# Dealing out the next group's x operands singly, loading two weight sets before the fixed tail, and loading the first group's weights a step sooner

## The chip, the cores and the metric

The kernel runs on one core of a Trainium2 chip. The metric is the device time of one execution, in microseconds (us). In this text TensorE is PE, VectorE is DVE, ScalarE is ACT, GpSimd is POOL, and SP is the engine that issues the DMA transfers. Each engine has a queue of its own and works through it in its program's order; an instruction that waits for a semaphore holds all that stands behind it on that engine.

## The reference

```python
# q, k, v: (8, 12, 448, 64) f32;  w_in: (768, 2048);  w_out: (2048, 768)
scores = (q @ k.T) / sqrt(64) - log(448)
attn = sigmoid(scores) @ v
x = attn.transpose(0, 2, 1, 3).reshape(8 * 448, 12 * 64)   # 3584 tokens x 768
h = x @ w_in
r = maximum(h, 0)
out = (r * r) @ w_out
```

## The kernel before

The attention comes first (until about 249.7 us) and leaves x in DRAM (`xd`), transposed. Then comes the MLP over four groups of tokens, `GROUPS`: three of 2 x 512 tokens and a last one of 2 x 256, here called groups 0 to 3. Each group has two matrix products, `gemm1` (x by w_in, L566) and `gemm2` (relu squared, by w_out, L678). Both are done by a 2 x 2 block scheme with seven products in the place of eight, numbered 1 to 7, whose operands are sums and differences of blocks.

Every f32 operand is split into a rounded high half and a low rest: `split_to` (L344) casts on ACT (the row `L345 ACT CAST`) and subtracts on DVE (`L347 DVE TENSOR_TENSOR`). A product of two split operands takes three matmuls (`product`, L558): high by high, high weights by low x, low weights by high x. So a weight set or an x operand can be used only when its DMA has landed, its cast is done on ACT and, for the second or third matmul, its subtraction is done on DVE.

**gemm1** runs 56 steps, each of one product n and one chunk i of eight, written (n, i), of 9 matmuls. `STEPS` gives their order. Weights come in kinds: A for products 1 and 2, B for 6 and 7, C for 3 and 5, D for 4. `w1C_1_6` is kind C, group 1, chunk 6; the trace drops the numbers and calls it `w1C`. Its PE rows write `ha`, `hb` and `hc`. The last ten steps, the tail, are (1,7), (5,6), (2,7), (6,7), (3,6), (7,7), (5,7), (4,6), (3,7), (4,7). In groups 1 to 3 they stand in a fixed order written out by hand, with a list `work` of loads (`load`), splits of weights (`halve`) and splits of operands (`operand`) for the first product of `gemm2`, each behind a numbered tail step (L661 to L674). A loop ahead of it (L658) loads and halves A, B and C of chunk 7 and D of chunk 6. C of chunk 6, which (5,6) needs as the tail's second step, is loaded and halved in line, just ahead of that step.

**gemm2** runs its products in the order 1, 2, 6, 7, 5, 4, 3, each of 72 matmuls. Its PE rows write `oa`, `ob` and `oc`. While a product runs, the operands and weights of the next are made: `operand(n, j)` (L687) for j = 0 to 3. The operands of product 3 are called `o3_0` to `o3_3` here; the trace writes the halves of any product's j-th operand as `o_0h`, `o_0l` and so on, and the blocks that they are split from as `g`.

**The next group's x** is loaded and combined by `x_operands` (L356). It makes loads of four blocks, 11, 12, 22 and 21 (each an `x` tile of two thirds and a `y` tile of one third), and a dictionary of eleven pieces: 1, 2, t1, t2, 6, t3, 7, 5, 3, t4, 4. The numbers are splits of that product's operand, the t's are differences on DVE. Some of them overwrite a loaded block, so their order matters. `ahead` (L764) issues the loads and all eleven pieces at the start of product 4's part of the program, ahead of `operand(3, 0)`.

What sets the order: the attention and all of `gemm1` of group 0 are written in a fixed order. There, `between` gives the work behind each step: loads of weights (`load_first`) six steps ahead of their use, halves three steps ahead, and three deferred conversions of w_out chunks (`deferred`, L184), each with four loads, ACT and DVE work, and seven stores to DRAM (`store`, L210) at its end. `gemm2` and the first 46 steps of `gemm1` in groups 1 to 3 are ordered by a scheduler that goes by the order in which the program issues work, so what is issued first has the better place on ACT, DVE and SP.

The tiles come from pools with fixed numbers of buffers: 35 of two columns (`op2`: x tiles, operands, g blocks), 12 of one column (`op1`: y tiles, snaps, outputs) and 7 wide ones for weights (`wide`). A load waits until its buffer is free, so a weight load goes out when PE is done with the set that is seven loads back.

Of the kernel before, what the change touches and what calls it, by code (L numbers as in the profile page):

```python
# [64 lines left out]
PIECES = {7: (1,), 14: (3,), 21: (2,), 22: (6,)}  # L65
T_PIECES = {22: ("t1", "t2"), 23: ("t3",)}
FIRST_W1 = 20
PUTS_FIRST = (9, 17)


@with_exitstack
def sigmoid_attention_relu2_mlp(
# [111 lines left out]
    def deferred(i, at):  # L184


        f, a, s = {}, {}, {}

        def load(n, u, k):
            t = op2(f"fd{n}_{i}").rearrange("p a s -> p (a s)")[:, : 2 * HALF]  # L190
            nc.sync.dma_start(out=t.bitcast(I32), in_=w_out[u][:, k * HALF : (k + 1) * HALF].bitcast(I32))
            f[n] = t.rearrange("p (n w) -> p n w", w=2)

        def block(n):
            return op1(f"b{n}_{i}")[:, :HALF]

        def words(n):
            a[n] = block(n)
            convert_upper(f[n], a[n])
            convert_lower(f[n], a[n])  # L200

        def add_up():
            for n in (5, 6, 7, 3):
                s[n] = block(n)
            nc.vector.tensor_add(out=s[5], in0=a[0], in1=a[4])
            nc.vector.tensor_sub(out=s[6], in0=s[5], in1=a[1])
            nc.vector.tensor_sub(out=s[7], in0=a[1], in1=a[0])
            nc.vector.tensor_sub(out=s[3], in0=a[2], in1=s[6])

        def store():  # L210
            for n, t in (a | s).items():
                if n:
                    nc.sync.dma_start(out=w2[i][:, PLACE[1][n]], in_=t)

        out = []
        for b, (n, u, k) in enumerate(((1, i, 0), (0, i, 1), (4, i + NI, 0), (2, i + NI, 1))):
            out.append((at + 3 * b - 5, lambda n=n, u=u, k=k: load(n, u, k)))
            out.append((at + 3 * b, lambda n=n: words(n)))
            out.append((at + 3 * b + 1, lambda n=n: convert_join(f[n], a[n])))
        out.append((at + 12, add_up))  # L220
        out.append((at + 13, store))
        return out

    def load_weights(src, name):
# [309 lines left out]
    def load_first(i, kind):  # L534
        first[i, kind] = load_w1(0, i, kind)
# [30 lines left out]
    def gemm1(g, ops, weights, between):  # L566

        T = GROUPS[g][1]
        blocks, operands, second = {}, {}, {}
        banks, snaps = {}, {}

        def tile_of(n, i):
            if (n, i // 2) not in blocks:
                blocks[n, i // 2] = op2(f"g{n}_{g}_{i // 2}", n=T)
            return blocks[n, i // 2][:, i % 2]

        def squares(n, i, scalar=False):  # L580
            if i % 2 == 0:
                return
            t = blocks[n, i // 2]
            if scalar:
                if n != "12":
                    nc.scalar.activation(t, t, AF.Relu)
                nc.scalar.activation(t, t, AF.Square)
            else:
                nc.vector.scalar_tensor_tensor(out=t, in0=t, scalar=0.0, in1=t, op0=ALU.max, op1=ALU.mult)

        pending = []

        def squares_later(n, i):

            if g == 0:
                pending.append(lambda: squares(n, i, scalar=True))
            else:
                squares(n, i)

        def flush(count):  # L600
            for _ in range(count):
                pending.pop(0)()

        def snap(k, i):
            s = snaps[k, i] = op1(f"s{k}_{g}_{i}", n=T)
            nc.scalar.copy(out=s, in_=banks["a", i])  # L606

        def run(n, i):
            count = len(pending)
            kind, at = SPOT[n]  # L610
            if (i, kind) not in weights:
                weights[i, kind] = halve_weights(load_w1(g, i, kind))
            k = {1: "a", 6: "a", 5: "a", 3: "a", 7: "b", 4: "b", 2: "c"}[n]
            if n in (1, 7, 2):
                banks[k, i] = bank(f"h{k}_{g}_{i}")[:, :T]
            out = banks[k, i]
            hi, lo = weights[i, kind]
            w = tuple(t[:, at].rearrange("p (c m) -> p c m", m=P) for t in (hi, lo))
            for c in range(NE):
                product(out, w, c, ops[n][c], n in (1, 7, 2) and c == 0, c == NE - 1)  # L620
            if n == 1:
                snap(1, i)
            elif n == 2:
                nc.vector.tensor_add(out=tile_of("11", i), in0=out, in1=snaps[1, i])
                squares("11", i)
            elif n == 6:
                snap(2, i)
            elif n == 5:
                snap(4, i)
                nc.vector.tensor_add(out=tile_of("22", i), in0=banks["b", i], in1=snaps[4, i])  # L630
                squares_later("22", i)
            elif n == 3:
                nc.scalar.activation(tile_of("12", i), out, AF.Relu)
                squares("12", i, scalar=True)
                if i % 2:
                    t, o = blocks["12", i // 2], blocks["11", i // 2]
                    nc.vector.tensor_sub(out=t, in0=t, in1=o)
            elif n == 4:
                nc.vector.tensor_add(out=tile_of("21", i), in0=out, in1=snaps[2, i])
                squares_later("21", i)  # L640
            flush(count)

        def operand(j):
            operands[j] = split(blocks["11", j], f"o1_{g}_{j}", lambda *name: op2(*name, T))

        def load(j):
            second[j] = load_w2(g, 1, j)

        def halve(j):
            halve_weights(second[j])  # L650

        head, tail = STEPS[g > 0][:-TAIL], STEPS[g > 0][-TAIL:]
        for at, (n, i) in enumerate(head):
            run(n, i)
            for work in between.get(at, ()):
                work()
        if g > 0:
            for i, kind in ((NI - 1, "A"), (NI - 1, "B"), (NI - 1, "C"), (NI - 2, "D")):  # L658
                if (i, kind) not in weights:
                    weights[i, kind] = halve_weights(load_w1(g, i, kind))  # L660
        work = [(1, load, 0), (3, load, 1), (4, halve, 0), (5, operand, 0), (6, operand, 1), (7, halve, 1)]  # L661
        if g > 0:
            work.append((0, lambda kind: weights.update({(NI - 1, kind): load_w1(g, NI - 1, kind)}), "D"))
            work.append((4, lambda kind: halve_weights(weights[NI - 1, kind]), "D"))
        with ExitStack() as fixed:
            if g > 0:
                fixed.enter_context(tc.manual_schedule())
            for at, (n, i) in enumerate(tail):
                run(n, i)
                for piece in between.get(len(head) + at, ()):  # L670
                    piece()
                for behind, piece, arg in work:
                    if behind == at:
                        piece(arg)  # L674
        flush(len(pending))
        return blocks, operands, second

    def gemm2(g, blocks, operands1, weights1, ahead):  # L678
# [51 lines left out]
        for j in range(NI // 2):  # L730
            operand(1, j)
        for at, n in enumerate(order):
            if n == 4:
                ahead()
            k = {1: "a", 6: "a", 5: "a", 3: "a", 7: "b", 4: "b", 2: "c"}[n]
            if n in (1, 7, 2):
                for e in range(NE):
# [1 line left out]
            for j in range(NI // 2):  # L739
                if at + 1 < len(order):  # L740
                    operand(order[at + 1], j)
                for e in range(NE):
                    for i in (2 * j, 2 * j + 1):
                        w = tuple(t[:, i % 2].rearrange("p (c m) -> p c m", m=P) for t in weights[n][j])
                        x = tuple(t[:, i % 2] for t in ops[n][j])
                        product(banks[k, e], w, e, x, n in (1, 7, 2) and i == 0, i == NI - 1)
# [14 lines left out]
                    put("21", e, 0, 6)  # L761

    def ahead_of(g):
        def ahead():  # L764
            if g < NG:
                ops[g], pieces = x_operands(g)
                for piece in pieces.values():
                    piece()

        return ahead  # L770

    with tc.manual_schedule():
# [45 lines left out]
            uses.setdefault((i, SPOT[product_][0]), n)  # L818
        for (i, kind), n in uses.items():
            if n >= 10 and (i, kind) not in first:  # L820
                work.append((n - 6, lambda i=i, kind=kind: load_first(i, kind)))
                work.append((n - 3, lambda i=i, kind=kind: halve_weights(first[i, kind])))
        for n, i in enumerate(DEFERRED):
            work += deferred(i, 6 + 11 * n)
        between = {}
# [2 lines left out]
        made = gemm1(0, ops[0], first, between)  # L828
    gemm2(0, *made, ahead_of(1))
    for g in range(1, NG):  # L830
        gemm2(g, *gemm1(g, ops[g], {}, {}), ahead_of(g + 1))


# [35 lines left out]
```

## Time and profile before

| | us |
|---|---|
| median of 3 runs | 1093.89 (1093.74 to 1094.51) |
| profiled execution | 1095.63 |
| its span, first to last instruction | 1093.9 |
| PE busy in it | 1065.7 (97%) |
| DVE busy | 799.9 (73%) |
| ACT busy | 652.9 (60%) |
| POOL busy | 72.9 (7%) |
| mean granted TensorE clock | 0.991 |

The span is what the trace covers; the profiled execution's time has 1.7 us more around it. Matmul ends are modelled, so a PE row's start is what to go by: back to back matmuls start at an even distance, and a larger one is lost time. The granted clock is a share of 2.4 GHz; the other level is 1.2 GHz, which reads 0.5. An idle time with `<-` names what the waiting instruction waited for last.

### The profile page before, as it was taken

What the parts mean: (1) busy time and instruction counts of PE and PEld (TensorE: products, weight loads), DVE (VectorE), ACT (ScalarE), POOL (GpSimd) and SP (SyncE); (2) the same over time, 40 slices, a digit from 0 to 9 for tenths busy, and PEclk for the clock granted to TensorE, in tenths of its full rate; (3) what the DMA queues carried; (4) which work ended last, traced back from release to release, by engine and by line L of the source; (5) the groups of instructions that cost most, each with busy time, mean ns of one, the idle gap of its engine ahead of it and who ended that gap; (6) DMA issues with size and microseconds to landing.
All of it is one profiled execution on the core that took longest, in us unless ns stands there. A gap on an engine that the chain in (4) does not pass through costs nothing.

```text
span 1093.9 us, 16699 instructions
## 1 busy us (share of the span) xinstructions
PE 1065.7 (97%) x6433; PEld 829.9 (76%) x6433; DVE 799.9 (73%) x1009; ACT 652.9 (60%) x910; POOL 72.9 (7%) x42
## 2 busy tenths in 40 slices
PE   9999999999999999979999999899999999999998
PEld 4555555557778888868887888778887888799898
DVE  5999989986776897574554996764555994747696
ACT  7899898885665865443443654533434663545664
POOL 1322322200120000000000000000000000000000
PEclk9999999999999999989999999999999999999999
DMA  9989999964464445533332445543333344556564
GB/s 356 380 298 332 351 391 346 329 218 142 143 233 139 124 121 178 168 96 107 102 101 72 116 129 166 167 123 87 89 100 95 106 124 148 154 165 184 169 194 128
DMA packets 90832, 196.13 MB, mean 179 GB/s; under 512 B 8320, under 2 KB 51712, under 8 KB 90752
## 3 DMA queue, kind: packets, MB, share of 16 engines
q1 hardware_dynamic: 90608, 195.00, 54.8%
q8 instruction: 50, 0.82, 0.3%
q14 instruction: 30, 0.25, 0.1%
q10 hardware_dynamic: 144, 0.07, 0.0%
HBM read 154.14 MB, written 40.89 MB: 178 GB/s over the span
## 4 chain that ended last, share of the span: by engine, by line
PE 62%; DVE 4%; DMA 3%; ACT 1%; issue 1%; SPq 0%; ACTq 0%; DVEq 0%
PE oa L562 20%; PE ha L562 17%; PE hb L562 9%; PE ob L562 6%; PE oc L562 5%; PE hc L562 4%; DMA w<-w 1%; DMA y<-xd 1%; DVE xlt L347 1%; DMA w1C<-w 1%; DVE x L375 1%; DVE yt L347 0%; DVE xl L347 0%; DVE y L347 0%; DVE y L375 0%
## 5 line engine op out<-in xcount | busy, mean ns | idle before, releaser
L347 DVE TENSOR_TENSOR w<-w 128x768 fp32r<-128x768 f32 x112 | 106.5, 953 | 60.3 <-ACT w L345 59.9
L345 ACT CAST w<-w 128x768 fp32r<-128x768 f32 x112 | 93.1, 835 | 92.1 <-DMA w<-w 85.7
L266 ACT ACTIVATE at<-sc 128x896 f32<-128x896 f32 x144 | 119.5, 941 | 6.7 <-PE sc L278 6.7
L606 ACT COPY s<-ha 128x512 f32<-128x512 f32 (+1 forms) x96 | 51.0, 533 | 114.0 <-PE ha L562 111.1
L309 PE MATMUL pav<-at,v 64*64 64x448 f32 x1152 | 118.1, 540 | 0.0
L309 PEld LDWEIGHTS pav<-at,v 64*64 64x64 f32 x1152 | 41.6, 133 | 60.8 <-issue 54.2
L516 DVE TENSOR_TENSOR ql<-x,qh 128x896 fp32r<-128x896 f32 x47 | 72.4, 1580 | 0.0
L562 PE MATMUL oa<-o_0h,w 128*128 128x512 f32 (+1 forms) x192 | 58.5, 379 | 11.6 <-ACT o_0h L345 11.6
L162 POOL TENSOR_TENSOR a<-a,f 128x768 int32<-128x768 int32 x26 | 58.1, 2235 | 163.8 <-DVE a L159 75.2
L347 DVE TENSOR_TENSOR w1A<-w1A 128x768 fp32r<-128x768 f32 x31 | 29.6, 955 | 39.3 <-ACT w1A L345 39.0
L278 PE MATMUL sc<-qh 64*128 64x448 f32 x282 | 54.2, 381 | 2.3 <-DVE xo L341 2.3
L562 PE MATMUL oa<-o_3h,w 128*128 128x512 f32 (+1 forms) x192 | 55.6, 363 | 0.0
L562 PE MATMUL oa<-o_1h,w 128*128 128x512 f32 (+1 forms) x192 | 55.6, 362 | 0.0
L562 PE MATMUL oa<-o_2h,w 128*128 128x512 f32 (+1 forms) x192 | 55.6, 362 | 0.0
L347 DVE TENSOR_TENSOR w1B<-w1B 128x768 fp32r<-128x768 f32 x31 | 30.1, 972 | 33.1 <-ACT w1B L345 33.1
L278 PE MATMUL sc<-qh,ql 64*128 64x448 f32 x282 | 51.5, 362 | 0.4 <-DVE ql L516 0.4
L278 PE MATMUL sc<-ql,qh 64*128 64x448 f32 x282 | 51.4, 361 | 0.0
L562 PEld LDWEIGHTS oa<-o_0h,w 128*128 128x128 f32 x192 | 36.4, 198 | 18.3 <-ACT o_0h L345 12.5
L347 DVE TENSOR_TENSOR w1C<-w1C 128x768 fp32r<-128x768 f32 x32 | 32.3, 1008 | 24.4 <-ACT w1C L345 24.4
L345 ACT CAST w1A<-w1A 128x768 fp32r<-128x768 f32 x32 | 26.7, 834 | 38.2 <-DMA w1A<-w 38.0
L562 PE MATMUL ha<-xht,w1C 128*128 128x512 f32 (+1 forms) x128 | 42.0, 374 | 7.3 <-ACT w1C L345 4.9
L345 ACT CAST w1C<-w1C 128x768 fp32r<-128x768 f32 x32 | 26.7, 835 | 37.0 <-DMA w1C<-w 37.0
(189 smaller groups left out, 2821.6 us busy)
## 6 DMA issues: line engine op xcount, KB each, us to landing
w<-w SPq DMA_DIRECT2D x112, 384.0 KB, 3.4
x<-qk SPq DMA_DIRECT2D x47, 448.0 KB, 6.5
f<-w_in SPq DMA_DIRECT2D x16, 768.0 KB, 9.0
w1A<-w SPq DMA_DIRECT2D x32, 384.0 KB, 3.2
w1B<-w SPq DMA_DIRECT2D x32, 384.0 KB, 3.2
w1C<-w SPq DMA_DIRECT2D x32, 384.0 KB, 3.5
v<-v SPq DMA_DIRECT2D x24, 448.0 KB, 7.0
w<-s SPq DMA_DIRECT2D x26, 384.0 KB, 8.5
```

The lines of the kernel that those rows point to most:

```text
L162: nc.gpsimd.tensor_tensor(out=wb, in0=wb, in1=t.bitcast(I32)[:, :, 0], op=ALU.add)
L266: nc.scalar.activation(at, sc, AF.Sigmoid, bias=NEG_LOG_S, scale=SCALE)
L278: nc.tensor.matmul(sc[:, j], x[kp][rows, 1, ks], x[qp][rows, 0], start=(n == 0), stop=(n == len(passes) - 1),)
L309: nc.tensor.matmul(sums[columns, h], vt[rows, n % 2 * NT + t, columns], at[t][rows, j], start=(t == 0 and (n % 2, h) != (1, 1)), stop=(t = ...
L345: nc.scalar.copy(out=hi, in_=raw)
L347: nc.vector.tensor_sub(out=lo, in0=raw, in1=hi.bitcast(F32))
L375: nc.vector.tensor_sub(out=o, in0=x, in1=y)
L516: nc.vector.tensor_sub(out=xs[n][1], in0=x[n], in1=xs[n][0].bitcast(F32))
L562: nc.tensor.matmul(out, a[:, c], b, start=first and n == 0, stop=last and n == 2, skip_group_check=True)
L606: nc.scalar.copy(out=s, in_=banks["a", i])
```

## The change

Three things are altered.

1. The next group's x. The loads of the four blocks are issued one product sooner, at the start of product 5's part. The eleven pieces no longer come at once. `AHEAD` deals out 1, 2, t1, t2 with 6, t3 and 7, each behind one `operand(3, j)` of product 4's part or one j of product 3's part; `BEHIND` puts 5, 3, t4 and 4 behind steps 0, 2, 4 and 5 of the next `gemm1`.
2. The tail of `gemm1` in groups 1 to 3. The loop ahead of the tail now takes A of chunk 7, C of chunk 6, B of chunk 7 and D of chunk 6. C of chunk 7 is loaded behind tail step 0 and halved behind 3; D of chunk 7 is loaded behind 3 (was 0) and halved behind 6 (was 4). The loads of product 1's first two weight sets of `gemm2` move from behind 1 and 3 to behind 2 and 5, their halves from 4 and 7 to 5 and 8, the two operand splits from 5 and 6 to 6 and 7. These latter moves hold for group 0's tail too.
3. Group 0's weights. Loads go seven steps ahead of their use (was six), halves four (was three), and the deferred conversions' stores go out four steps later.

```diff
--- before.py
+++ after.py
@@ -65,6 +65,10 @@
 PIECES = {7: (1,), 14: (3,), 21: (2,), 22: (6,)}
 T_PIECES = {22: ("t1", "t2"), 23: ("t3",)}
 FIRST_W1 = 20
+
+
+AHEAD = {2: (1,), 3: (2,), 4: ("t1",), 5: ("t2", 6), 6: ("t3",), 7: (7,)}
+BEHIND = {0: (5,), 2: (3,), 4: ("t4",), 5: (4,)}
 PUTS_FIRST = (9, 17)
 
 
@@ -218,7 +222,7 @@
             out.append((at + 3 * b, lambda n=n: words(n)))
             out.append((at + 3 * b + 1, lambda n=n: convert_join(f[n], a[n])))
         out.append((at + 12, add_up))
-        out.append((at + 13, store))
+        out.append((at + 17, store))
         return out
 
     def load_weights(src, name):
@@ -655,13 +659,18 @@
             for work in between.get(at, ()):
                 work()
         if g > 0:
-            for i, kind in ((NI - 1, "A"), (NI - 1, "B"), (NI - 1, "C"), (NI - 2, "D")):
+            for i, kind in ((NI - 1, "A"), (NI - 2, "C"), (NI - 1, "B"), (NI - 2, "D")):
                 if (i, kind) not in weights:
                     weights[i, kind] = halve_weights(load_w1(g, i, kind))
-        work = [(1, load, 0), (3, load, 1), (4, halve, 0), (5, operand, 0), (6, operand, 1), (7, halve, 1)]
+        def load_last(kind):
+            weights[NI - 1, kind] = load_w1(g, NI - 1, kind)
+
+        def halve_last(kind):
+            halve_weights(weights[NI - 1, kind])
+
+        work = [(2, load, 0), (5, load, 1), (5, halve, 0), (6, operand, 0), (7, operand, 1), (8, halve, 1)]
         if g > 0:
-            work.append((0, lambda kind: weights.update({(NI - 1, kind): load_w1(g, NI - 1, kind)}), "D"))
-            work.append((4, lambda kind: halve_weights(weights[NI - 1, kind]), "D"))
+            work = [(0, load_last, "C"), (3, halve_last, "C"), (3, load_last, "D"), *work, (6, halve_last, "D")]
         with ExitStack() as fixed:
             if g > 0:
                 fixed.enter_context(tc.manual_schedule())
@@ -730,8 +739,8 @@
         for j in range(NI // 2):
             operand(1, j)
         for at, n in enumerate(order):
-            if n == 4:
-                ahead()
+            if n == 5:
+                ahead(None)
             k = {1: "a", 6: "a", 5: "a", 3: "a", 7: "b", 4: "b", 2: "c"}[n]
             if n in (1, 7, 2):
                 for e in range(NE):
@@ -739,6 +748,8 @@
             for j in range(NI // 2):
                 if at + 1 < len(order):
                     operand(order[at + 1], j)
+                if n in (4, 3):
+                    ahead((n == 3) * NI // 2 + j)
                 for e in range(NE):
                     for i in (2 * j, 2 * j + 1):
                         w = tuple(t[:, i % 2].rearrange("p (c m) -> p c m", m=P) for t in weights[n][j])
@@ -761,11 +772,14 @@
                     put("21", e, 0, 6)
 
     def ahead_of(g):
-        def ahead():
+        def ahead(at):
             if g < NG:
-                ops[g], pieces = x_operands(g)
-                for piece in pieces.values():
-                    piece()
+                if at is None:
+                    ops[g], made = x_operands(g)
+                    pieces.clear()
+                    pieces.update(made)
+                else:
+                    pieces_of(*AHEAD.get(at, ()))
 
         return ahead
 
@@ -818,8 +832,8 @@
             uses.setdefault((i, SPOT[product_][0]), n)
         for (i, kind), n in uses.items():
             if n >= 10 and (i, kind) not in first:
-                work.append((n - 6, lambda i=i, kind=kind: load_first(i, kind)))
-                work.append((n - 3, lambda i=i, kind=kind: halve_weights(first[i, kind])))
+                work.append((n - 7, lambda i=i, kind=kind: load_first(i, kind)))
+                work.append((n - 4, lambda i=i, kind=kind: halve_weights(first[i, kind])))
         for n, i in enumerate(DEFERRED):
             work += deferred(i, 6 + 11 * n)
         between = {}
@@ -828,7 +842,8 @@
         made = gemm1(0, ops[0], first, between)
     gemm2(0, *made, ahead_of(1))
     for g in range(1, NG):
-        gemm2(g, *gemm1(g, ops[g], {}, {}), ahead_of(g + 1))
+        between = {n: [lambda names=names: pieces_of(*names)] for n, names in BEHIND.items()}
+        gemm2(g, *gemm1(g, ops[g], {}, between), ahead_of(g + 1))
 
 
 def kernel(q, k, v, moe_w_in, moe_w_out):
```

**ACT, end of gemm2 of group 0.** Before, the splits of product 3's operands (`o3_...`) stand behind the casts of all x operands (`xh`, `yt` and so on) of group 1:

```order
L345 CAST w1B_1_0_5042<-w1B_1_0_5042 128x768
L345 CAST yt1_1_4799<-y12_1_4750 128x512
L345 CAST xh22_1_4804<-x22_1_4753 128x1024
L345 CAST y22_1_4806<-y22_1_4754 128x512
L345 CAST xht4_1_4813<-x21_1_4757 128x1024
L345 CAST w1A_1_1_5067<-w1A_1_1_5067 128x768
L345 CAST yt4_1_4815<-y21_1_4758 128x512
L345 CAST o3_0_0h_4820<-g22_0_0_3316 128x1024
L345 CAST o3_0_1h_4846<-g22_0_1_3540 128x1024
L345 CAST o3_0_2h_4872<-g22_0_2_3802 128x1024
L345 CAST o3_0_3h_4898<-g22_0_3_4026 128x1024
```

After, they stand in product 5's stretch, among the casts of product 4's weights and the snaps of product 7 (`t7`), with only two x casts (`xh11`, `y11`) ahead of the last one:

```order
L349 CAST o3_0_0h_4763<-g22_0_0_3318 128x1024
L349 CAST w2_0_4_0_4651<-w2_0_4_0_4651 128x768
L349 CAST o3_0_1h_4789<-g22_0_1_3542 128x1024
L736 COPY t7_0_0_4622<-ob_0_0_4515 128x512
L349 CAST o3_0_2h_4815<-g22_0_2_3797 128x1024
L736 COPY t7_0_1_4624<-ob_0_1_4516 128x512
L349 CAST w2_0_4_1_4678<-w2_0_4_1_4678 128x768
L349 CAST xh11_1_4823<-x11_1_4628 128x1024
L736 COPY t7_0_2_4626<-ob_0_2_4517 128x512
L349 CAST w2_0_4_2_4705<-w2_0_4_2_4705 128x768
L349 CAST y11_1_4825<-y11_1_4629 128x512
L349 CAST o3_0_3h_4848<-g22_0_3_4028 128x1024
```

The four splits moved up by 20 to 28 places; `o3_3` now stands behind the cast of `y11`.

**SP, end of gemm1 of group 1.** Before, C of chunk 6 is the last weight load of the tail, behind D of chunk 7 and ahead of product 1's weights (`w2_1_1_...`):

```order
L228 DMA w1A_1_7_5646<-w1 128x768
L228 DMA w1B_1_7_5650<-w1 128x768
L228 DMA w1C_1_7_5654<-w1 128x768
L228 DMA w1D_1_6_5658<-w1 128x384
L228 DMA w1D_1_7_5676<-w1 128x384
L228 DMA w1C_1_6_5678<-w1 128x768
L228 DMA w2_1_1_0_5695<-w2 128x2x384
```

After, it stands second among the last loads of chunk 7, and C and D of chunk 7 come later:

```order
L232 DMA w1A_1_7_5646<-w1 128x768
L232 DMA w1C_1_6_5650<-w1 128x768
L232 DMA w1B_1_7_5654<-w1 128x768
L232 DMA w1D_1_6_5658<-w1 128x384
L232 DMA w1C_1_7_5676<-w1 128x768
L232 DMA w2_1_1_0_5703<-w2 128x2x384
L232 DMA w1D_1_7_5718<-w1 128x384
```

So `w1C_1_6` moved four places up, `w1C_1_7` two places down, and D of chunk 7 behind the first of product 1's loads.

**ACT, group 0, around (5,4) and (6,5).** Before, the cast of `w1B_0_5` stands behind the relu and the square of block g21:

```order
L345 CAST w1C_0_4_3683<-w1C_0_4_3683 128x768
L148 ACTIVATE b0_7_3764<-fd0_7_3667 128x384
L151 ACTIVATE fd0_7_3667<-fd0_7_3667 128x384
L606 COPY s1_0_5_3777<-ha_0_5_3767 128x512
L586 ACTIVATE g21_0_1_3628<-g21_0_1_3628 128x1024
L587 ACTIVATE g21_0_1_3628<-g21_0_1_3628 128x1024
L345 CAST w1B_0_5_3719<-w1B_0_5_3719 128x768
L606 COPY s4_0_4_3800<-ha_0_4_3634 128x512
```

After, it follows the cast of `w1C_0_4`, ahead of them and of the snap of (1,5):

```order
L349 CAST w1C_0_4_3664<-w1C_0_4_3664 128x768
L349 CAST w1B_0_5_3704<-w1B_0_5_3704 128x768
L152 ACTIVATE b0_7_3761<-fd0_7_3669 128x384
L155 ACTIVATE fd0_7_3669<-fd0_7_3669 128x384
L610 COPY s1_0_5_3774<-ha_0_5_3764 128x512
L590 ACTIVATE g21_0_1_3628<-g21_0_1_3628 128x1024
L591 ACTIVATE g21_0_1_3628<-g21_0_1_3628 128x1024
L610 COPY s4_0_4_3795<-ha_0_4_3638 128x512
```

The cast moved five places up. On SP, two loads of this stretch (`w1C_0_3`, `w1B_0_4`) that stood behind the seven stores of the first deferred chunk now stand ahead of them.

## Rows read from the trace of the kernel before

**Rows 1.** The page's first part: busy time of each engine, its share of the span, and its instructions.
```profile
PE 1065.7 (97%) x6433; PEld 829.9 (76%) x6433; DVE 799.9 (73%) x1009; ACT 652.9 (60%) x910; POOL 72.9 (7%) x42
```

**Rows 2.** The waits of PE by what was waited for: us in total, times, longest.
```profile
PE oa L562 <- ACT o_0h L345: 11.6, 2, 5.8
PE ha L562 <- ACT w1C L345: 4.9, 3, 2.0
PE ha L562 <- DVE w1C L347: 2.5, 4, 1.5
PE oa L562 <- DVE o_0l L347: 1.6, 1, 1.6
```

**Rows 3.** Busy time of the engines in four stretches around PE's waits: the stretch, its length, busy time of PE, PEld, DVE, ACT and POOL, granted clock, DMA share, GB/s.
```profile
466.00:478.00 12.00, 6.15 (x19) 4.44 (x18) 12.00 (x14) 8.44 (x11) 0.00 (x0) 0.72 0.12 33
586.00:594.00 8.00, 6.34 (x20) 4.47 (x19) 2.18 (x3) 1.90 (x3) 0.00 (x0) 0.79 0.13 43
946.00:950.00 4.00, 2.37 (x10) 1.61 (x10) 4.00 (x6) 3.38 (x4) 0.00 (x0) 1.00 0.42 122
1015.00:1024.00 9.00, 6.46 (x39) 6.05 (x39) 3.68 (x7) 1.79 (x4) 0.00 (x0) 0.81 0.35 100
```

**Rows 4.** The chain that ended last, in order of time: start, us, what. `oa x72` at 368.31, 608.76, 848.51 and 1030.22 is the first product of `gemm2` in groups 0 to 3; 913.79 is product 5 of group 2, 964.67 the first step of group 3's `gemm1`.
```profile
368.31 16.32 PE oa L562 x72
...
584.55 2.05 PE ha L562 x9
...
587.11 0.84 ACT w1C L345
...
587.97 0.97 DVE w1C L347
...
594.48 4.08 PE ha L562 x18
...
608.76 16.32 PE oa L562 x72
...
848.51 16.32 PE oa L562 x72
...
913.79 12.25 PE oa L562 x54
...
964.67 1.07 PE ha L562 x9
...
1012.72 1.09 PE hb L562 x9
...
1013.83 3.21 DMA w1C<-w
...
1030.22 8.67 PE oa L562 x72
1038.89 8.64 PE oc L562 x72
```

**Rows 5.** The timeline at the change from group 0's `gemm2` to group 1's `gemm1`, PE, SP and DVE: start, us, engine, line, operation, out<-in, count, and in brackets the idle time before it and what ended it. The y loads, the first DVE piece of x, product 3's first low half, and PE's last matmul before and first after the wait.
```profile
466.75 0.39 PE L562 MATMUL hb<-xlt,w1B 128*128 128x512 f32 x1
472.99 1.65 PE L562 MATMUL oa<-o_0h,w 128*128 128x512 f32 x3 [5.85 <-ACT o_0h L345]
...
452.11 1.88 SPq L370 DMA_DIRECT2D y<-xd x4
...
456.14 0.69 DVE L347 TENSOR_TENSOR y<-y,y 128x512 fp32r<-128x512 f32 x1 [1.00 <-ACT y L345]
...
473.00 1.22 DVE L347 TENSOR_TENSOR o_0l<-g,o_0h 128x1024 fp32r<-128x1024 f32 x1
```

**Rows 6.** The timeline of SP and ACT: the load of `w1C_1_6` in the tail of group 1 and of `w1C_3_6` in that of group 3, and there a snap on ACT.
```profile
582.54 0.32 SPq L228 DMA_DIRECT2D w1C<-w  x1
...
1013.83 0.32 SPq L228 DMA_DIRECT2D w1C<-w  x1
...
1015.99 0.37 ACT L606 COPY s<-ha 128x256 f32<-128x256 f32 x1 [1.65 <-PE ha L562]
```

**Rows 7.** The timeline of group 0: PE's first matmul of (1,3) and of (3,2) four steps later, of (5,4) and of (3,4) three steps later; the ACT cast and the DVE subtraction that came late for (6,5) and (5,4).
```profile
286.64 0.39 PE L562 MATMUL ha<-xh,w1A 128*128 128x512 f32 x1
...
296.23 0.39 PE L562 MATMUL ha<-xh,w1C 128*128 128x512 f32 x1
...
318.82 0.39 PE L562 MATMUL ha<-xht,w1C 128*128 128x512 f32 x1
...
327.13 0.39 PE L562 MATMUL ha<-xh,w1C 128*128 128x512 f32 x1
...
323.54 0.82 ACT L345 CAST w1B<-w1B 128x768 fp32r<-128x768 f32 x1
...
319.90 0.95 DVE L347 TENSOR_TENSOR w1C<-w1C 128x768 fp32r<-128x768 f32 x1
```

**Rows 8.** The timeline in product 7 of group 0: the low half of product 5's first operand on DVE, and two loads of product 5's weights on SP.
```profile
407.66 1.22 DVE L347 TENSOR_TENSOR o_0l<-g,o_0h 128x1024 fp32r<-128x1024 f32 x1
...
417.35 4.46 SPq L228 DMA_DIRECT2D w<-w  x2
```

**Rows 9.** DMA issues by group: out<-in, queue, operation, count, KB of one, median us from issue to landing.
```profile
w<-w SPq DMA_DIRECT2D x112, 384.0 KB, 3.4
...
x<-xd SPq DMA_DIRECT2D x8, 512.0 KB, 4.6
```

## The prediction

> **What bounds the kernel now.** I read the busy times first: PE is busy for 1065.7 us, 97% of the span [rows 1], so only what keeps PE from starting its next matmul, or slows its clock, can be won. The waits of PE come next: nearly all of it stands in four groups, product 3's first operand (11.6 us in two waits on ACT, 1.6 in one on DVE) and the weights `w1C` (4.9 and 2.5 us) [rows 2]. The windows then show a cost that the wait list lacks: behind some waits the granted clock is low, 0.72 over 466 to 478 us and 0.79 over 586 to 594 [rows 3]; since the lower level is 0.5, the first means (1 - 0.72) x 12 / 0.5 = 6.7 us at half rate. The chain gives the measure for all of it: 72 matmuls of 512 columns take 16.32 us, 0.2267 each, a step of nine 2.04; at 256 columns 8.64, 0.12 and 1.08 [rows 4]. What a stretch takes above that is what can be won there, waits and clock together.
>
> **The stretches.** From the first product of group 0's `gemm2` to that of group 1 there are 1008 matmuls, 228.48 us, and the trace has 608.76 - 368.31 = 240.45: 11.97 us lost. For group 1 to 2 it is 848.51 - 608.76 = 239.75: 11.27 lost [rows 4]. The tail's share is read from 584.55 to 594.48: 9.93 us for three steps, 6.12, so 3.81 lost; the remaining 8.16 and about 7.46 lie at the change of groups. In the third change, 913.79 to 964.67 is 50.88 us for three products, 48.96: 1.92 lost. Group 3's tail, from 1012.72 to 1030.22, is 17.50 for twelve steps, 12.96: 4.54 lost [rows 4]. In group 0, 286.64 to 296.23 is 9.59 for four steps, 8.16, and 318.82 to 327.13 is 8.31 for three, 6.12: 1.43 and 2.19 lost [rows 7]. Together 11.97 + 11.27 + 1.92 + 4.54 + 3.62 = **33.3 us**. Each belongs to one part of the change.
>
> **Part 1, the x operands.** At 466.75 PE has done product 4 and four early matmuls of the next group, then stands until 472.99, 5.85 us idle, for `o3_0`. DVE is why: it started the x pieces at 456.14, when y had landed (issued at 452.11), was busy without a gap from 466 to 478, and came to `o_0l` at 473.00 [rows 3, 5]. The change removes no instruction; it moves eleven pieces behind the four `o3` splits, which have only blocks from `gemm1` as inputs. On ACT they now stand among the casts of product 4's weights. The latest of them, `o3_3`, stands behind the cast of `y11`, whose load follows a weight load that goes out when product 7 ends, 368.31 + 4 x 16.32 = 433.6. In the trace y was there, and cast, 4.0 us after its issue (452.11 to 456.14), so by about 438 here, and the split is done by about 441, an estimate, against a need at 433.6 + 2 x 16.32 = 466.2 and later. These 25 us hold the 16.9 that DVE took for all pieces (456.14 to 473.00). So the wait and the slow clock behind it go: 8.16 + 7.46 + 1.92 = 17.54.
>
> What is late next? The pieces that have gone behind. Product 3 now ends at about 482.5. The new group's product 6 is needed two steps later, 486.6, and its operand is done by about 476 (pieces of 1.22 and 0.69 us on DVE, [rows 5], from about 441 on, in the gaps between the weights' halves); 5, 3 and 4 are needed at about 492.7, 498.8 and 502.9, and each has at most 3.8 us of DVE work. I cost them at nothing, covered by PE's own steps; without that cover each would cost its lateness, a few us. On SP, the two loads of `x11` and `x12` now stand ahead of a load of product 5's weights, and wait for op2 buffers that product 7's and 5's splits free: the one at 407.66 to 408.88 [rows 8]. The weights behind them went out at 417.35 and are used at 433.6 + 8.16 = 441.75: no cost.
>
> **Part 2, the tails.** `w1C_1_6` was issued at 582.54 because it was the last in SP's queue for a step that begins at 586.6; cast at 587.11, subtracted at 587.97 to 588.94 [rows 4, 6]. A weight load waits for PE to be done with the set seven loads back; by PE's steps its new place, four loads up, goes out about 14 us before that. What is late next is C of chunk 7, now issued at about 580.5 and needed 16 us later, and D of chunk 7, issued at about 584.5, halved after (5,7) and done by about 602.9, with (4,7) due at 603.4 on the old clock: 0.5 us to spare, an estimate from PE's steps and the halves' 0.84 and 0.97. So 3.81 goes in each of two tails, which is in the 11.97 and 11.27.
>
> Group 3's steps are half as long and the loads aren't, so there the spare is thin. `w1C_3_6` was issued at 1013.83 [rows 6] for (5,6), due at 1012.72 + 3 x 1.08 = 1016.0; four loads up it goes out about 7 us sooner. C of chunk 7 goes out a step ahead of the old load, at about 1012.7, and with its 3.2 [rows 4] lands by 1016. Its cast stands behind the snap of (6,7), a step that without a wait ends at about 1019.1: snap 0.37 [rows 6], cast 0.84 and subtraction 0.97 [rows 4] give 1021.2, and (5,7)'s third matmul wants it at about 1021.4. D of chunk 7 comes out at 1024.9 against 1025.0, and product 1's second weight set some 0.25 us late, since its cast has gone behind a relu and a square in ACT's order. I charge 0.25 for the last and, for two margins below 0.25, 0.35 more: **0.6 us** off the 4.54, an estimate. The bounds are 0 (all margins hold) and 4.5 (all of the old loss comes back).
>
> **Part 3, group 0.** The late work is of the kind of the DVE subtraction at 319.90, done at 320.85 for a matmul due two places after 318.82, 319.3, and of the ACT cast at 323.54, done with its subtraction at about 325.3 for one due at 323.4 without the earlier wait [rows 7]: 1.6 and 1.9 us late. Halves move a step, 2.04 us, up, and that cast also passes a relu and a square. The stores that moved back by four steps no longer stand ahead of `w1C_0_3` on SP. So I take all 3.62; the other bound is 0, if ACT and DVE come to the halves no sooner because something ahead of them still waits for PE.
>
> **Sum.** 33.3 - 0.6 = 32.7. Against the profiled execution's own 1095.63: 1062.9. The runs' median is 1093.89, 1.74 lower, and PE's waits are the same program's in each, so I take the sum from it: **1061.2 us**.
>
> **Rivals.** (a) Group 3's tail still waits. For: margins of 0.1 to 0.2 us, worked out on durations that vary by that. Against: nothing there is queued for longer than a step. It gives back 1 to 4.5 us, 1062 to 1065.7. Whether a short wait pays a slow clock too the rows leave open: 2.3 us at most, from (1,7)'s end at 586.60 to 588.94, were followed by a mean of 0.79 [rows 3, 4], the 1.6 for `o_0l` in 946 to 950 by 1.00 [rows 2, 3]. The Trainium skill ("TensorE: Matmul & The Clock Gate", section "HAM oscillation — how this bites in real kernels") describes a kernel in which every wait for a load put PE back to 1.2 GHz, so that the work behind it started cold; by that (a) would lie at its upper end, 1065.7, and the wait in 946 to 950 should have cost clock, which its row denies. (b) Group 0's halves stay where they are in time, since ACT and DVE come to them no sooner: 3.6 back, 1064.8. For: what stands ahead of a half in those queues waits for PE's own steps; against: the order now puts behind them the work that they stood behind. (c) The change of groups waits again for something else, `y11` in front of `o3_3` or a piece of the next group: up to 8.16 for one, 7.46 more for two: 1069.4 or 1077. (d) Slower: SP stops at `x11` and holds product 5's weights. It decides from the point at which an op2 buffer comes free later than 438.3 (441.75 less the 3.4 of such a load [rows 9]); then PE waits in product 5 in all three changes. It takes more than 32.7 / 3 = 10.9 us in each, so a buffer free at 449 or later, to end above 1093.9; free at 450, it costs 11.7 in each and gives 1061.2 + 35.1 = 1096.3. The trace has the split that frees it at 408.88, which speaks against it. The Trainium skill ("DMA: Bandwidth & Descriptors", section "Queues, rings and completion order") says that each DMA engine takes its descriptors in the order of the ring, so that two x loads ahead also push back the landing of those weights; by the 4.6 us of such a load [rows 9] that is at most 9.2, to about 430, still before 441.75. (e) Part 1 doesn't do what it says, because the scheduler puts the `o3` splits back behind the pieces in one of the changes or in all: up to 17.5 back, 1078.7. Against: the order of ACT shows them ahead.
>
> **How the numbers follow.** Forecast 0.60 (1059.5 to 1063), a 0.19, b 0.07, c 0.06 (most of it one change of groups), d 0.05, e 0.03. The low end is all 33.3 and the 0.5 to 1 us of small gaps beside it won: 1059.5. The high end takes in a, b and one change of groups of c: 1069.5. That leaves out part of c, d and e, about 0.1. A measurement of this kernel tells about 0.2%, 2.2 us, from no change. Faster by more 0.95; d, by the length of its hold, gives 0.02 within and 0.03 slower.
>
> **What would show it.** Right: product 3 follows product 4 without a gap in all three changes, the granted clock stays at 1.00 there and in the tails, the wait list holds no `o_0h` and no `w1C` above 0.5 us, and the two distances between first products come to about 228.5. Wrong: a wait for `w` in product 5 (d), one for `xht` or `yt` early in a `gemm1` (c), for `w1C` or `w1D` after (6,7) in group 3 (a), or for `w1A` to `w1C` before 368 (b).

## The result and the profile after

The median went from 1093.82 to **1064.01 us** (1063.87 to 1065.81 in four runs), a ratio of 0.973, 95% interval 0.9713 to 0.9747. The forecast was 1061.2 in 1059.5 to 1069.5: the direction and the range held, and 29.8 us were won where 32.7 were forecast. The profiled execution took 1065.81 us, its span is 1064.0, and the granted clock is 1.000 on the mean (before: 0.991).

The waits of PE in the changed kernel: us in total, times, longest.

```profile
PE sc L282 <- DVE xo L345: 2.3, 2, 1.2
PE hb L566 <- DVE w1D L351: 1.2, 1, 1.2
PE warm_ps L791 <- DVE warm L411: 1.2, 1, 1.2
PE oa L566 <- ACT w L349: 0.5, 1, 0.5
PE sc L282 <- DVE ql L520: 0.3, 1, 0.3
PE ha L566 <- ACT s L610: 0.2, 1, 0.2
```

All four groups of [rows 2] are gone. What is left in the MLP is a wait for `w1D`, one for product 1's weights and one for a snap; the waits for `sc` and `warm_ps` lie in the attention and at the start.

The same windows as in [rows 3], moved to the same places of the program (the change from group 0 to 1, the tail of group 1, the end of group 3's `gemm1`):

```profile
462.00:474.00 12.00, 12.00 (x55) 9.94 (x54) 9.36 (x12) 5.82 (x9) 0.00 (x0) 1.00 0.48 143
580.00:595.00 15.00, 13.61 (x59) 10.60 (x58) 8.96 (x11) 10.24 (x15) 0.00 (x0) 1.00 0.46 129
...
990.00:1004.00 14.00, 13.45 (x108) 12.87 (x108) 10.54 (x17) 9.94 (x18) 0.00 (x0) 1.00 0.70 208
```

At the change of groups PE is busy for all of 12 us, where it was 6.15, and the clock column reads 1.00 everywhere.

The chain that ended last, the lines that answer to [rows 4]: products 5, 4 and 3 of group 0, and the first products of groups 0 to 2 (`oc` is the second).

```profile
364.17 16.32 PE oa L566 x72
...
429.44 16.32 PE oa L566 x72
445.76 16.32 PE ob L566 x72
462.08 16.32 PE oa L566 x72
...
594.64 16.33 PE oa L566 x72
...
823.38 16.34 PE oa L566 x72
839.72 16.32 PE oc L566 x72
...
1008.71 8.64 PE oc L566 x72
```

Product 3 begins where product 4 ends (445.76 + 16.32 = 462.08), and the starts of PE's matmuls show no gap at the other two changes of groups either. From first product to first product it is 594.64 - 364.17 = 230.47 and 823.38 - 594.64 = 228.74 us, against the 228.48 of 1008 matmuls: 1.99 and 0.26 lost, where it was 11.97 and 11.27. From second product to second product, 839.72 to 1008.71 is 168.99 for six products of 16.32, 56 steps of 1.08 and one product of 8.64, 167.04: 1.95 lost, most of it at the end of group 3's `gemm1`. Group 0 shows no wait at all.

The 1.99 of group 1 is one story, and the chain tells it:

```profile
582.48 4.85 DMA w<-w
...
587.40 0.85 ACT w L349
...
588.28 0.96 DVE w L351
589.24 0.61 DVE g L634
...
591.01 1.03 DVE o_0l L351
...
592.15 0.56 DVE w1D L351
...
592.75 1.89 PE hb L566 x7
```

The load issued at 582.48 is that of product 1's third weight set, `w2_1_1_2`. It is no part of the hand-written tail, but the scheduler set its cast between the tail's pieces on ACT, ahead of the snap of (5,7) (ACT's copy of that step's result, L610), of the first operand's cast and of that of D of chunk 7. ACT stood 3.60 us for it; then the snap, the sum that needs the snap, `o_0l` and at last `w1D` came late, and (4,7) waited until 592.75.

To compare traces below, "lost" is the sum of what the starts of successive matmuls in the MLP lie apart above 226.7 ns (512 columns) or 120 ns (256). For the kernel before it is 34.3 us, for the changed kernel 4.3.

### The profile page after: what moved, and what is told of

Same layout as the page of the kernel before. It is cut to its first block, busy times and chain, and to the rows that moved or that the text cites. A ratio compares the mean times of both kernels' runs of the same rounds, so it can differ in the third digit from the quotient of the medians.

```text
span 1064.0 us, 16715 instructions
## 1 busy us (share of the span) xinstructions
PE 1054.8 (99%) x6433; PEld 824.9 (78%) x6433; DVE 798.8 (75%) x1009; ACT 650.8 (61%) x910; POOL 72.4 (7%) x42
## 4 chain that ended last, share of the span: by engine, by line
PE 95%; DVE 3%; DMA 1%; ACT 0%; issue 0%; SPq 0%; ACTq 0%; DVEq 0%
PE oa L566 22%; PE ha L566 21%; PE ob L566 11%; PE hb L566 10%; PE pav L313 10%; PE sc L282 8%; PE hc L566 5%; PE oc L566 5%; PE pav L325 2%; PE sr L298 1%; DMA w<-w 1%; DVE ql L520 1%; DMA x<-qk 1%; DVE a L163 0%; DVE qh L516 0%
## 5 line engine op out<-in xcount | busy, mean ns | idle before, releaser
L610 ACT COPY s<-ha 128x512 f32<-128x512 f32 (+1 forms) x96 | 51.0, 532 | 102.9 <-PE ha L566 99.2
L566 PE MATMUL oa<-o_0h,w 128*128 128x512 f32 (+1 forms) x192 | 55.7, 363 | 0.0
L593 DVE SCALAR_TENSOR_TENSOR g<-g 128x1024 f32<-128x1024 f32 (+1 forms) x40 | 42.5, 1064 | 1.1
L282 PEld LDWEIGHTS sc<-qh 64*128 64x128 f32 x282 | 26.4, 184 | 21.7 <-PE pav L313 16.2
L349 ACT CAST w1B<-w1B 128x768 fp32r<-128x768 f32 x32 | 26.7, 835 | 26.0 <-DMA w1B<-w 26.0
```

The source lines that it names most:

```text
L282: nc.tensor.matmul(sc[:, j], x[kp][rows, 1, ks], x[qp][rows, 0], start=(n == 0), stop=(n == len(passes) - 1),)
L349: nc.scalar.copy(out=hi, in_=raw)
L566: nc.tensor.matmul(out, a[:, c], b, start=first and n == 0, stop=last and n == 2, skip_group_check=True)
```

## The experiments

**One part at a time.** Three kernels are the kernel before with one of the three parts. Their edits are pieces of the change; the core of each:

```diff
# part1
-            if n == 4:
-                ahead()
+            if n == 5:
+                ahead(None)
...
+                if n in (4, 3):
+                    ahead((n == 3) * NI // 2 + j)
# part2
-            for i, kind in ((NI - 1, "A"), (NI - 1, "B"), (NI - 1, "C"), (NI - 2, "D")):
+            for i, kind in ((NI - 1, "A"), (NI - 2, "C"), (NI - 1, "B"), (NI - 2, "D")):
...
+            work = [(0, load_last, "C"), (3, halve_last, "C"), (3, load_last, "D"), *work, (6, halve_last, "D")]
# part3
-        out.append((at + 13, store))
+        out.append((at + 17, store))
...
-                work.append((n - 3, lambda i=i, kind=kind: halve_weights(first[i, kind])))
+                work.append((n - 4, lambda i=i, kind=kind: halve_weights(first[i, kind])))
```

> The kernel before with part 1 alone, the x pieces dealt out behind the splits of product 3's operands. Theory: the losses at the three changes of groups are worth 8.16 + 7.46 + 1.92 = 17.5 us, clock included, and nothing of them hangs on the other parts: 1093.8 - 17.5 = 1076.3 us, with product 3 following product 4 without a gap and the losses of the tails (3.8, 3.8, 4.5 us) and of group 0 (3.6) still there. Rival: the parts overlap, so that a tail whose neighbours changed loses more; then 1077.5 or more.

> The kernel before with part 2 alone, the new order of loads and halves in the tails. Theory, from the trace of the changed kernel: what is left there (1.9 us in the tail of group 1, 1.4 at the end of group 3's) comes from this part's own order on ACT, where the cast of product 1's third weight set stands ahead of the cast of w1D of chunk 7 and waits for its DMA; so the gain is at most 3.8 + 3.8 + 4.5 less 1.4 = 10.7 and with group 1's wait 8.8: 1083.1 to 1085.0 us. Rival: that wait is the x pieces' doing (part 1), and part 2 alone wins 12 us: 1081.8 or less.

> The kernel before with part 3 alone, group 0's weights a step sooner and the deferred stores later. Theory: 3.6 us, 1090.2, and no wait of PE between 250 and 365 us. Rival: the halves come no sooner because something ahead of them on ACT and DVE still waits for PE, and 1093 or more.

| kernel | median us | ratio to before (1093.55 here), interval | won | lost in its trace |
|---|---|---|---|---|
| part 1 | 1076.61 | 0.9845 (0.9826 to 0.9863) | 16.9 | 16.2 |
| part 2 | 1085.64 | 0.9926 (0.9907 to 0.9946) | 7.9 | 25.3 |
| part 3 | 1089.47 | 0.9967 (0.9955 to 0.9978) | 4.1 | 29.0 |

The parts add up: 16.9 + 7.9 + 4.1 = 28.9 against 29.8 together, within the intervals. Part 1 takes the waits for `o_0h` and `o_0l` out, part 2 those for `w1C` in the tails, part 3 those of group 0, and each leaves the others'. Part 3's 3.6 came out as 4.1, so rival (b) is out. Part 2 at 1085.64 lies 0.6 above its expected range. No run takes the edits inside part 2 or part 3 apart (loads, halves and, in part 3, the stores), so which of them was needed isn't shown. Part 2's trace still loses 0.4, 0.4 and 1.2 us in the three tails, 10.1 less than the 12.1 that they lost in the trace of before, as the theory had it and not the 12 of its rival; yet the median moved by 7.9 only. The trace of part 1, whose tails are those of before, shows why. Its windows over the tails of groups 1, 2 and 3 (columns as in [rows 3]):

```profile
577.00:585.00 8.00, 6.33 (x20) 4.51 (x19) 2.50 (x3) 1.90 (x3) 0.00 (x0) 0.79 0.18 49
809.00:817.00 8.00, 6.33 (x27) 4.59 (x27) 3.21 (x5) 1.90 (x3) 0.00 (x0) 1.00 0.18 50
995.00:1005.00 10.00, 7.22 (x46) 6.81 (x45) 4.36 (x8) 1.90 (x4) 0.00 (x0) 0.83 0.33 92
```

PE's timeline in the same trace, the waits in these two tails:

```profile
579.42 0.50 PE L566 MATMUL ha<-xht,w1C 128*128 128x512 f32 x1 [1.41 <-ACT w1C L349]
580.41 1.22 PE L566 MATMUL ha<-xht,w1C 128*128 128x512 f32 x2 [0.26 <-DVE w1C L351]
...
811.75 0.50 PE L566 MATMUL ha<-xht,w1C 128*128 128x512 f32 x1 [1.41 <-ACT w1C L349]
812.74 0.73 PE L566 MATMUL ha<-xht,w1C 128*128 128x512 f32 x2 [0.26 <-DVE w1C L351]
```

The waits are alike to the hundredth, 1.41 and 0.26 us. Behind the first the clock fell (0.79), behind the second it didn't (1.00); the tails lose 3.8 and 2.2 us. In part 3's trace neither fell. So the 3.8 per tail that the prediction took from one trace is 2.2 of wait and a half rate that comes or stays away. In the traces where the clock stays up in both, the tails of groups 1 to 3 lose 2.2, 2.2 and 4.6 to 4.8; of that part 2, which leaves 2.0, can win some 7.

**Which half of part 1 counts.** Two more kernels take the loads and the order apart. In the first the x loads and all pieces come at once, as before, but behind the splits of product 3's operands; in the second the loads go out a product sooner and the pieces stay ahead of those splits (`ahead(5)` issues the loads, `ahead(4)` all pieces).

```diff
# o3_first
-            if n == 4:
-                ahead()
...
                     operand(order[at + 1], j)
+                if n == 4 and j == NI // 2 - 1:
+                    ahead()
# x_sooner
-            if n == 4:
-                ahead()
+            if n in (5, 4):
+                ahead(n)
```

> The kernel before with one edit: the x loads and all eleven pieces are issued at once as before, but behind the four splits of product 3's operands and not ahead of them; nothing is loaded sooner and nothing dealt out. Theory: the order alone did it, since the pieces still have from 456 to 486 us for 16.9 us of DVE work: 17.5 us as in part 1, 1076.3, within 1. Rival: the earlier loads are needed, and without them the new group's operands come late for the first steps of its gemm1, so that several us of wait move there: 1080 to 1090.

> The kernel before with one edit: the x loads go out one product sooner, the eleven pieces stay where they were, ahead of the splits of product 3's operands. Theory: the wait was a matter of the pieces' start (456 us, when y had landed) and of the order together, and either cure is enough: y is there by about 438, the 17 us of pieces and the halves between them end before product 4 does (466), so that the three changes lose at most 1 us each: 1076 to 1079. Rival: only the order counts, since ACT comes to the last pieces behind the cast of product 3's last weights, whose buffer PE frees late; several us of wait remain at each change: 1082 to 1093.

They took 1076.17 us (0.984, 0.9817 to 0.9863) and 1075.70 (0.9835, 0.982 to 0.985), the same as part 1's 1076.61. The chain of the first at the change from group 0 to 1, products 4 and 3 and the first steps of group 1:

```profile
449.51 16.32 PE ob L562 x72
465.83 16.32 PE oa L562 x72
482.15 2.04 PE ha L562 x9
484.19 2.04 PE hc L562 x9
486.23 2.04 PE ha L562 x9
```

No gap, though DVE still works through the x pieces from 455.92 to 471.90: they have product 3's own 16 us to hide in. The second has no gap there either (product 3 at 465.02, 16.32 behind product 4 at 448.70), with the pieces ahead of the splits and some 18 us sooner (the first split of a y tile at 437.50, before at 456.14). So the wait needed both, late pieces and splits queued behind them, and either cure is enough. Dealing the pieces out singly won nothing beyond that; both rivals, that the order alone or the early loads are needed, are out.

**Group 1's tail.** Does the late third weight set come back each time, and is its place in ACT's queue the cause? The changed kernel again, and two kernels that pin the third and fourth weight set behind the last tail step in groups 1 and 2; the last also halves D of chunk 7 ahead of the first operand's split in groups 1 to 3, and the second weight set a step sooner in all four.

```diff
# pin and pin_order, groups 1 and 2
+        if 0 < g < NG - 1:
+            work += [(8, load, 2), (9, load, 3), (9, halve, 2), (9, halve, 3)]
# pin_order, beside that
-        work = [(2, load, 0), (5, load, 1), (5, halve, 0), (6, operand, 0), (7, operand, 1), (8, halve, 1)]
+        work = [(2, load, 0), (5, load, 1), (5, halve, 0), (6, operand, 0), (7, halve, 1), (7, operand, 1)]
...
-            work = [(0, load_last, "C"), (3, halve_last, "C"), (3, load_last, "D"), *work, (6, halve_last, "D")]
+            work = [(0, load_last, "C"), (3, halve_last, "C"), (3, load_last, "D"), (6, halve_last, "D"), *work]
```

> The changed kernel as it is, to see whether the 1.9 us in group 1's tail come back. If the landing of product 1's third weight set (4.85 us there, 3.1 in group 2) is a matter of chance, this trace shows 0.2 to 0.5 us there and the median stays at 1064 within 0.5; if it is the program's, 1.9 us stand there again.

> The changed kernel with one addition in groups 1 and 2: the loads and halves of product 1's third and fourth weight set get a place in the fixed tail, behind its last step, so that their casts can no longer stand ahead of the snap of (5,7) and of w1D of chunk 7. Theory: that cast, waiting for its DMA, is what holds ACT in group 1's tail; the wait goes, 1.3 to 1.9 us, 1062 to 1062.7. Rival: the snap and w1D are late because of the splits ahead of them, and nothing changes or the later halves make product 1 wait: 1064 or more.

> As the run before it, and in all tails w1D of chunk 7 is halved ahead of the split of product 1's first operand, and product 1's second weight set one step sooner. Theory: this takes the 0.1 to 0.3 us in front of (4,7) and the 0.9 us in front of product 1's second weight set in group 3: 1061 to 1062, the least of all. Rival: the halves change places with pieces that PE needs as soon, and it stays within 0.5 us of the run before it.

> The changed kernel a third time. Theory: the loss in group 1's tail goes with the landing of product 1's third weight set on ACT: 0.4 to 0.6 us where it lands within 3.4 us of its issue, over 1 where it takes over 4. Rival: it has another cause, and a long loss stands beside a short landing or the other way round.

> As the run before it, a fourth trace of the changed kernel: the same two readings of group 1's tail, and of group 2's beside it.

| kernel | us | load of the third weight set to landing, group 1 | lost in group 1's tail | lost in all |
|---|---|---|---|---|
| changed, first trace | 1064.01 median | 4.85 | 1.93 | 4.3 |
| changed, after_c | 1064.64 (one run) | 3.81 | 0.93 | 3.3 |
| changed, after_again | 1064.12 median | 3.42 | 0.54 | 2.5 |
| changed, after_b | 1063.42 (one run) | 3.40 | 0.51 | 2.8 |
| pin | 1062.85 median | not in the chain | 0.0 | 2.1 |
| pin_order | 1061.75 median | not in the chain | 0.0 | 1.5 |

The landings are the lines of the chains of after_c, after_again and after_b:

```profile
582.21 3.81 DMA w<-w
```

```profile
582.14 3.42 DMA w<-w
```

```profile
581.52 3.40 DMA w<-w
```

The loss follows the landing one to one: 1.45 us more of landing, from 3.40 to 4.85, and 1.42 more of loss. So the long wait differs from execution to execution of one program, for a reason that no run shows, and a remainder of 0.5 is the program's. Pinned behind the tail, the casts hold nothing up. The chain of `pin_order` through group 1's tail is PE alone:

```profile
582.16 2.04 PE hb L566 x9
584.21 2.04 PE ha L566 x9
586.25 2.04 PE hb L566 x9
588.28 2.04 PE ha L566 x9
590.33 2.04 PE hb L566 x9
592.37 7.71 PE oa L566 x34
```

Beside the changed kernel on the same chip (1064.12, 0.9734, 0.972 to 0.9747), `pin` has 1062.85 (0.9719, 0.9706 to 0.9732) and `pin_order` 1061.75 (0.9709, 0.9696 to 0.9722). The intervals overlap, so the step to `pin` alone is not settled by the times, and 1062.85 lies a little above the 1062 to 1062.7 expected; its trace shows the wait gone. `pin_order` is the fastest version, by 0.2%, and its runs (1061.12 to 1062.08) lie below every run of the changed kernel (1063.39 and up). Its only wait of PE in the MLP is this:

```profile
PE oa L566 <- DVE w L351: 0.2, 1, 0.2
```

**The kernel before, again.** The sum was made on one trace. Two more traces of the same program:

> The kernel before once more, for a second trace of the same program. Theory: the waits in the tails of groups 1 and 2 (1.4 and 0.3 us) come back, but the half rate behind them is chance, since one of the traces of part 1 shows it in group 1 alone and that of part 3 in neither: a tail then loses 2.2 us and not 3.8, and the execution's time moves with the number of falls, 1.6 us each. Rival: the unchanged program falls into half rate in both tails each time, 3.8 and 3.8, and the profiled execution's distance to the median, 1.7 us, is what profiling adds.

> As the run before it, a third trace: by the theory at least one of the two shows a tail of group 1 or 2 that loses about 2.2 us; by the rival both show 3.8 in both.

They took 1093.43 and 1092.95 us, with 32.6 and 32.0 us lost, against 1095.63 and 34.3 in the trace that the prediction read. The windows over the tails of groups 1 and 2 in the first of them:

```profile
585.00:593.00 8.00, 6.34 (x27) 4.59 (x26) 3.20 (x4) 1.90 (x3) 0.00 (x0) 1.00 0.17 49
824.00:832.00 8.00, 6.33 (x27) 4.63 (x26) 3.24 (x4) 1.90 (x3) 0.00 (x0) 1.00 0.17 49
```

Both tails lose 2.2 and the clock stays at 1.00 there, in the second trace too; at the first two changes of groups it fell each time. The rival, that the half rate belongs to the program and the 1.7 us are what profiling adds, is out as far as the tails go.

## Why the prediction was right, and where 2.9 us went

Parts 1 and 3 came as worked out: 17.5 and 3.6 us were booked, 16.9 and 4.1 were won by each alone. The mechanism of part 1 held too: in the changed kernel's trace the last split of product 3's operands ends at 437.03, 7.6 us after product 7 (7.4 by the prediction) and 25 before product 3. Nothing new was late at the changes of groups: neither the first operands of the new group nor product 5's weights behind the x loads, so rivals (c), (d) and (e) did not come about, and the range held.

The 1064.0 lies above the 1059.5 to 1063 to which the forecast gave 0.60. What is missing lies in part 2, for which the sum has 3.81 + 3.81 + 4.54 - 0.6 = 11.6 us and which won 7.9 alone. Three sizes in it were wrong, all to the same side.

The step that was mis-sized first is the sum's last one: "I take the sum from" the median, with losses read in an execution that was 1.74 us longer than it. I held the 1.74 to lie outside of PE's waits. Part of it was in them: the half rate behind two short waits, 1.6 us each, which that trace had in both tails and eight of twelve tails with the same waits in other traces had not. Against it stands the change from group 1 to 2, where that trace lost 7.4 us and the other two of the kernel before 8.2 and 8.3: the granted clock was 0.86 over its 710 to 722 us and 0.72 over their 707 to 719. Of the 33.3 us, some 1.5 were not there to be won in a median run (34.3 lost in that trace, 32.0 and 32.6 in the other two of the kernel before, whose executions took 1092.95 and 1093.43).

The second is part 2's "0.5 us to spare" for D of chunk 7 in groups 1 and 2. It was reckoned on the tail's hand-written pieces alone, and the scheduler had set a cast that waits for a DMA between them. Instead of 0 the tail of group 1 keeps 0.5 to 1.9 us and that of group 2 0.2 to 0.4. For the four traces the two together average 1.3; 0.9 is what a run with a short landing keeps.

The third is group 3's tail, rival (a) in its small form: charged 0.6, it keeps 0.9 to 1.4. Two of its margins all but held (C of chunk 7 cost 0.06 us, D of chunk 7 0.2); product 1's second weight set was the larger share, in the first trace 0.5 of wait and 1.1 with what follows, where 0.25 was charged. Here too a scheduler's cast is the cause as far as the traces tell: between the tail's pieces on ACT it set the casts of the third and fourth weight sets (`w2_3_1_2` and `w2_3_1_3`), ahead of the second operand's cast, the relu, the square and the cast of the second set. ACT and PE in the changed kernel, from the fourth set's cast to the second set's first use:

```profile
998.63 0.83 ACT L349 CAST w<-w 128x768 fp32r<-128x768 f32 x1 [0.99 <-DVE g L643]
999.37 0.62 ACT L349 CAST o_1h<-g 128x512 fp32r<-128x512 f32 x1
999.89 0.38 ACT L637 ACTIVATE g<-ha 128x256 f32<-128x256 f32 x1
1000.30 0.63 ACT L591 ACTIVATE g<-g 128x512 f32<-128x512 f32 x1
1000.84 0.81 ACT L349 CAST w<-w 128x768 fp32r<-128x768 f32 x1
...
1001.70 0.39 PE L566 MATMUL oa<-o_1h,w 128*128 128x256 f32 x1 [0.54 <-ACT w L349]
```

The first of these casts stood for its load and for a step on DVE, done at 998.55 and 998.56. ACT's idle time before it is 0.99, 0.93, 0.81 and 0.58 us in the four traces of the changed kernel, and PE's loss at that first use is 0.3 less each time: 0.70, 0.62, 0.51 and 0.27. `pin_order`, which casts the second set a step sooner, doesn't have this loss. No half rate came of it.

Together 1.5 + 0.9 + 0.5 = 2.9 us, the distance from 32.7 to 29.8. The split is an estimate from the traces: the 0.9 and the 0.5 are read there, and the 1.5 is what they leave over, beside the 1.7 and 2.3 us by which the losses of the three traces of the kernel before differ.

## What to carry to other kernels

Where PE waits for a split that is queued behind work with a later due time, either let that work start earlier or put it behind; both did the same here, and dealing it out finely added nothing. A fixed order written by hand holds only its own pieces: look in the built order for what a scheduler has put between them, above all for a cast that waits for a transfer, and give those pieces a place as well. Before a loss that includes a fall of the clock is booked as a gain, look at a second trace of the same program.

## What the runs showed of the hardware that was not expected

The same pair of waits, 1.41 and 0.26 us with the same work before and after, was followed by a granted clock of 0.79 over 8 us in one tail and by 1.00 in the other of the same execution. The kernels that keep this wait (before in three traces, part 1, part 3, `o3_first` and `x_sooner`) have fourteen such tails of groups 1 and 2; six lost 3.8 us and eight 2.2. The waits of about 6 us at the first two changes of groups were followed by half rate in each of the five traces that have them, and the one of 1.3 to 1.9 at the last change in none of them. In group 3's tail, where the wait for `w1C` is 1.9 to 2.3 us, half rate followed in all seven traces that have it.

The same load of 384 KB, at the same place of the same program, landed 3.40, 3.42, 3.81 and 4.85 us after its issue in four executions.
